# Tile 0 of a linear attention and rational feed-forward kernel: float32 products that read their moving operand plainly

## The chip, the cores and the metric

The kernel runs on one core of one Trainium2 chip. The metric is the device time of that core in microseconds (us), the median of 3 runs. A profiled execution of the same program, taken separately, gives the rows that are quoted below.

## The reference

q, k and v have the shape (batch 8, heads 8, sequence 576, head width 64). The result is 4608 tokens by 512 columns, float32.

```python
kv = np.einsum('bhsd,bhse->bhde', k, v)
out = np.einsum('bhsd,bhde->bhse', q, kv)
rms = np.sqrt(np.mean(out * out, axis=-1, keepdims=True) + 1e-06)
x = out / rms * g_norm                      # then laid out as (4608, 512)
h = x @ w_in                                # (512, 2048)
P = a[0] + a[1] * h + a[2] * h**2 + a[3] * h**3
Q = 1.0 + np.abs(b[0]) * np.abs(h) + np.abs(b[1]) * h**2
g = P / (Q + 1e-06)
result = (g @ w_out).astype(np.float32)     # (2048, 512)
```

The weights w_in and w_out are float64 and are turned into float32 on the chip.

## The kernel before

The 4608 tokens are worked in 9 tiles of 512 (t), and the 2048 inner columns in 16 chunks of 128 (c). A pair (t, c) is a slot; the slots run in one list, and slot i of tile 0 has c = i. For each slot TensorE makes h, a PSUM tile of 128 inner columns by 512 tokens (gemm1_part), ACT, DVE and POOL turn it into g (ew_a, ew_b, ew_c, ew_d), and TensorE adds the slot's products with w_out to four PSUM banks acc, one for each 128 tokens (gemm2). In turn i TensorE gets gemm2 of slot i-2, the attention steps that prepare the next tile, and gemm1 of slot i+1; in the first four turns gemm1 stands ahead of the attention steps. h has two banks, so gemm1 of slot i+1 waits until slot i-1 has been read for the last time (L511).

The elementwise work of a slot passes to and fro: ACT L501 and L502 read h; DVE L504 and L505; ACT L510; DVE L511; ACT L513 and L514 (a logarithm and an exponential); DVE L520, L521 and L527, which gives g. Between these stand the steps of a plan written by hand (first_tiles, L153 to L178, read by todo at L185): in tile 0 and the start of tile 1 they turn the float64 words of both weight matrices into float32 (scale L209 and L211, shift L232, or L237, add L242) and split them into two float32r parts (cast L249, rest L269). An entry as "add P 5q" names the engine and the turn and place. All engines work their queues in order.

Most products are made of three float32r products of split operands (L493, L558). In tile 0 some are not split and run as float32, which takes two passes over the moving operand, each a record of its own with its own weight load: gemm1 of slots 0 to 3 (unsplit1, L486, 4 products each) and gemm2 of slots 0 to 11 (unsplit2, L551, 4 products each). gemm2 of slots 12 to 15 of tile 0 is split (L558, 12 products each).

The host stores the tokens of each tile of q, and the columns of w_out, with the even ones first and the odd ones behind them. The moving operand is read through strands, which takes column 0, 256, 1, 257 and so on, so that h and acc come out in natural order:

```python
    def strands(f):
        return f.rearrange("p (a b) -> p b a", a=2)
```

Other places read such an operand plainly: the first tile's attention output (first_o, L669, float32) and the later tiles' attention (att_o, L389 to L391, float32r, in two runs of stored order). When a tile's gemm2 is complete, evacuate copies acc to SBUF and stores it; for tile 0 that stands in turn 17 behind gemm2 of slot 15, and all four copies are ACT's (L567). gemm2 of tile 1's first slot (slot 16) writes the same four banks.

Of the kernel before, what the change touches and what calls it, by code (L numbers as in the profile page):

```python
# [23 lines left out]
def linear_attention_then_rational_ffn(  # L24
# [10 lines left out]
    PE, ACT, DVE, POOL = nc.tensor, nc.scalar, nc.vector, nc.gpsimd  # L35

    NB, NPAIR = kv.shape[:2]
    NT, DM = out.shape
    NF = w_in.shape[0]
    P = 128  # L40
# [79 lines left out]
    def unsplit1(t, c):  # L120
        return t == 0 and c < 4
# [4 lines left out]
    def unsplit2(t, c):  # L126
        return t == 0 and c < SPLIT0
# [61 lines left out]
    raws, ups, w32, whl, wparts = {}, {}, {}, {}, {}  # L189
# [130 lines left out]
    kvq, qs, sqs, rs, rbs, xf = {}, {}, {}, {}, {}, {}  # L320
# [52 lines left out]
    def halves(f):  # L373
        return f.rearrange("p (a b) -> p a b", a=2)
# [86 lines left out]
    acc = {}  # L461
# [6 lines left out]
    def in_turn(behind, n):  # L468
        each = [(k, j) for k in range(n) for j in range(3) if j != behind]
        return each if behind is None else each + [(k, behind) for k in range(n)]  # L470

    def strands(f):
        return f.rearrange("p (a b) -> p b a", a=2)

    def gemm1(t, c):
        if t == NTILE - 1 and c % 3 == 2:
            ph = ps_at.tile([P, TW], F32, tag="at", name=f"h_{t}_{c}", bufs=1)
        else:
            ph = ps_h.tile([P, TW], F32, tag="h", name=f"h_{t}_{c}")
        gemm1_part(t, c, ph)  # L480
        return ph

    def gemm1_part(t, c, ph, kcs=range(NPAIR)):
        if unsplit1(t, c):
            for kc in kcs:
                PE.matmul(ph, w32["wi", c][:, kc * P:(kc + 1) * P], strands(xf[t, kc]), start=(kc == 0), stop=(kc == NPAIR - 1))  # L486
            return
        order = in_turn(behind1.get((t, c)), NPAIR)
        for n, (kc, j) in enumerate(order):
            xh, xl = (strands(f) for f in x[t][kc])  # L490
            wh, wl = (f[:, kc * P:(kc + 1) * P] for f in whl["wi", c])
            w, f = ((wh, xh), (wl, xh), (wh, xl))[j]
            PE.matmul(ph, w, f, start=(n == 0), stop=(n == len(order) - 1))  # L493
# [23 lines left out]
    def ew_c(t, c, fill=lambda k: None):  # L517
        q, u, r = pend[t, c]
        fill(0)
        DVE.scalar_tensor_tensor(u, u, na[:, 0:1], r, ALU.add, ALU.mult)  # L520
        DVE.scalar_tensor_tensor(r, q, QEPS, r, ALU.add, ALU.mult)  # L521
        fill(1)
        if unsplit2(t, c):
            g = gs[t, c] = work.tile([P, TW], F32, tag=("gh", "gl")[c % 2], name=f"g_{t}_{c}")
        else:
            g = u
        DVE.scalar_tensor_tensor(g, r, 2.0, u, ALU.subtract, ALU.mult)  # L527
        fill(2)

# [14 lines left out]
    def gemm2(t, c):  # L544
        g = gs.pop((t, c))
        first, last = c == 0, c == NF - 1
        if first:
            acc[t] = [ps_acc.tile([P, DM], F32, tag="acc", name=f"acc_{t}_{s}") for s in range(NSUB)]
        if unsplit2(t, c):
            for s in range(NSUB):  # L550
                PE.matmul(acc[t][s], g[:, s * P:(s + 1) * P], strands(w32["wo", c]), start=first, stop=last)  # L551
            return
        (gh, gl), (wh, wl) = g, whl["wo", c]
        products = (gh, wh), (gh, wl), (gl, wh)
        order = in_turn(behind2.get((t, c)), NSUB)
        for n, (s, j) in enumerate(order):
            a, w = products[j]
            PE.matmul(acc[t][s], a[:, s * P:(s + 1) * P], strands(w), start=first and j == 0, stop=last and all(k != s for k, _ in order[n + 1:]))  # L558

    def evacuate(t):  # L560
        for k in range(NSUB // 2):
            ob = work.tile([P, 2, DM], F32, tag="rb", name=f"ob_{t}_{k}", bufs=2)
            for s in range(2):
                if s and 2 < t + 2 < NB:
                    DVE.tensor_copy(ob[:, s], acc[t][2 * k + s])
                else:
                    ACT.copy(ob[:, s], acc[t][2 * k + s])  # L567
            r0 = t * TW + 2 * k * P
            nc.sync.dma_start(out[r0:r0 + 2 * P].rearrange("(s p) d -> p s d", s=2), ob)

    def finish(t, ph):
# [12 lines left out]
        for k, (v, q, u, gh, gl, r) in zip(parts, halves):  # L584
# [4 lines left out]
            ACT.activation(r, q, AF.Ln, bias=bias[:, 2:3], scale=QSC)  # L589
            ACT.activation(r, r, AF.Exp, bias=bias[:, 3:4], scale=-1.0)  # L590
        gemm2(t, c - 2)
        for v, q, u, gh, gl, r in halves:
            DVE.scalar_tensor_tensor(u, u, na[:, 0:1], r, ALU.add, ALU.mult)
# [173 lines left out]
    scale_low(("wi", 2), ACT, two)  # L767
    h00 = ps_h.tile([P, TW], F32, tag="h", name="h_0_0")
    gemm1_part(0, 0, h00, (0,))
    first_rb(1)  # L770
    first_warm(3, 1)
# [5 lines left out]
    first_norm(3)  # L777
    scale_high(("wi", 2), DVE, two)
    gemm1_part(0, 0, h00, (1,))
    conv_b2(("wi", 0), two)  # L780
    first_rb(2)
# [10 lines left out]
    ph = h00  # L792
# [22 lines left out]
    for i, (t, c) in enumerate(slots[:-1]):  # L815
# [8 lines left out]
        if i >= LAG:  # L824
            gemm2(*slots[i - LAG])
            if slots[i - LAG][1] == NF - 1:
                evacuate(slots[i - LAG][0])
        if i < 4:
            ph = gemm1(0, i + 1)
        if t + 1 < NTILE:  # L830
# [4 lines left out]
            if i == MOVE[0]:  # L835
                last = work.tile([P, 2 * DM], F32, tag="rb", name="w_last", bufs=2)
# [6 lines left out]
        if t == NTILE - 1:  # L843
            ahead += [gemm1(*slots[k]) for k in ((i + 1, i + 2) if c == 0 else (i + 2,)) if k < len(slots)]
            ph = ahead.pop(0) if ahead else None
        elif i >= 4:
            ph = gemm1(*slots[i + 1])
        if c == NF - 2 and 0 < t < NTILE - 1:
            xl = [split(t + 1, p) for p in range(NPAIR)]
            for k in range(2):  # L850
                rest[k].append(xl[k])
                rest[2].append(xl[2 + k])
        ew_c(t, c, lambda k: [todo(i, "rgz"[k]), *(f() for f in rest[k])])
    finish(NTILE - 1, ph)

# [43 lines left out]
```

## Time and profile before

| what | value |
|---|---|
| median of 3 runs | 867.98 us (867.84 to 868.21) |
| the profiled execution: its own time, its span | 868.07 us, 866.3 us |
| PE busy, share of the span | 853.2 us, 98% |
| PE weight loads | 696.0 us, 80% |
| DVE | 687.7 us, 79% |
| ACT | 699.3 us, 81% |
| POOL | 328.1 us, 38% |
| granted TensorE clock | 1.000 |

The span goes from the first to the last instruction of the profiled execution; 1.8 us of its own time lie outside. Records of matmuls overlap, because each carries the time in which its results drain: the spacing of their starts is what one costs in a row of several. The chain of waits follows the work that ended last back from the end, at each step to what released it.

### The profile page before, as it was taken

Reading aid. Unit: us, or ns where it says so; the run is one execution under the profiler, and the core shown is the slowest. Engines: PE = TensorE matmul, PEld = TensorE weight load, DVE = VectorE, ACT = ScalarE, POOL = GpSimd, SP = SyncE. Lnnn points to the kernel's source line nnn. Section 1 sums busy time; section 2 is a strip of 40 time slices with the busy share of each in tenths; the row PEclk is TensorE's granted clock in tenths of the full one; section 3 lists DMA queues with packets and bytes.
Section 4 is the critical chain, followed back from the end, with each engine's and each line's share of the span. In section 5 each row is a group of like instructions: output and inputs, shape, how many; then the busy total and the mean of one; then the engine's idle time right before and its main releaser. Section 6 shows DMA issues by size and latency. Waiting matters only on the chain.

```text
span 866.3 us, 11993 instructions
## 1 busy us (share of the span) xinstructions
PE 853.2 (98%) x4370; PEld 696.0 (80%) x4370; DVE 687.7 (79%) x1022; ACT 699.3 (81%) x1129; POOL 328.1 (38%) x265
## 2 busy tenths in 40 slices
PE   8999999999999999999999999999999999999998
PEld 5355558888888888888888888888888888888886
DVE  3989998997887688768876887678877877787886
ACT  5988878897788678868886888868887788778875
POOL 3585555342433242424242423323332434142221
PEclk9999999999999999999999999999999999999999
DMA  9664262114010321132112202020112010101001
GB/s 358 274 250 169 98 213 62 62 37 147 26 61 27 133 50 48 37 135 50 49 37 99 85 3 71 25 50 2 61 37 49 2 61 25 33 18 49 1 1 49
DMA packets 24191, 65.93 MB, mean 76 GB/s; under 512 B 2372, under 2 KB 2756, under 8 KB 24132
## 3 DMA queue, kind: packets, MB, share of 16 engines
q1 hardware_dynamic: 23968, 65.04, 22.1%
q8 instruction: 34, 0.56, 0.3%
q14 instruction: 25, 0.20, 0.1%
q10 hardware_dynamic: 164, 0.14, 0.0%
HBM read 55.59 MB, written 9.57 MB: 75 GB/s over the span
## 4 chain that ended last, share of the span: by engine, by line
PE 61%; DVE 19%; ACT 17%; issue 2%; DMA 1%; SPq 0%; ACTq 0%; DVEq 0%
PE h L493 24%; PE acc L558 21%; PE acc L551 6%; ACT r L513 5%; ACT r L514 4%; DVE u L520 4%; ACT q L510 4%; DVE q L504 4%; DVE r L521 4%; DVE u L527 4%; PE h L486 2%; DVE x L316 2%; PE ms L344 2%; PE ms L410 1%; PE op L391 1%
## 5 line engine op out<-in xcount | busy, mean ns | idle before, releaser
L493 PE MATMUL h<-x,wiparts 128*128 128x512 f32 x1680 | 390.2, 382 | 0.0
L493 PEld LDWEIGHTS h<-x,wiparts 128*128 128x128 f32 x1680 | 315.2, 189 | 50.4 <-issue 4.1
L538 POOL TENSOR_TENSOR gl<-u,gh 128x512 fp32r<-128x512 f32 x131 | 170.7, 1303 | 411.7 <-ACT gh L537 338.1
L520 DVE SCALAR_TENSOR_TENSOR u<-u,na,r 128x512 f32<-128x512 f32 x143 | 106.9, 748 | 81.9 <-ACT r L514 81.5
L504 DVE SCALAR_TENSOR_TENSOR q<-v,b0abs,h 128x512 f32<-128x512 f32 x143 | 106.2, 742 | 57.7 <-ACT u L502 57.1
L501 ACT ACTIVATE v<-h,b 128x512 f32<-128x512 f32 x143 | 98.3, 688 | 55.8 <-PE h L493 53.4
L558 PE MATMUL acc<-woparts,gh 128*128 128x512 f32 x400 | 120.3, 380 | 3.5 <-ACT r L514 2.5
L558 PE MATMUL acc<-woh,gh 128*128 128x512 f32 x320 | 121.3, 379 | 0.0
L558 PE MATMUL acc<-woh,gl 128*128 128x512 f32 x320 | 121.3, 379 | 0.0
L558 PE MATMUL acc<-wol,gh 128*128 128x512 f32 x320 | 118.9, 379 | 0.4 <-POOL wol L269 0.4
L510 ACT ACTIVATE q<-q 128x512 f32<-128x512 f32 x143 | 90.3, 632 | 35.8 <-DVE q L504 33.9
L537 ACT CAST gh<-u 128x512 fp32r<-128x512 f32 x131 | 81.1, 619 | 44.7 <-DVE u L527 44.7
L511 DVE SCALAR_TENSOR_TENSOR u<-u,na,h 128x512 f32<-128x512 f32 x143 | 106.9, 748 | 5.1
L502 ACT ACTIVATE u<-h,na 128x512 f32<-128x512 f32 x143 | 110.9, 776 | 0.0
L513 ACT ACTIVATE r<-q,bias 128x512 f32<-128x512 f32 x143 | 99.1, 693 | 4.5
L521 DVE SCALAR_TENSOR_TENSOR r<-q,r 128x512 f32<-128x512 f32 x143 | 98.8, 691 | 0.0
L514 ACT ACTIVATE r<-r,bias 128x512 f32<-128x512 f32 x143 | 94.7, 662 | 4.6
L505 DVE TENSOR_TENSOR u<-u,h 128x512 f32<-128x512 f32 x143 | 97.4, 681 | 0.0
L527 DVE SCALAR_TENSOR_TENSOR u<-r,u 128x512 f32<-128x512 f32 x131 | 90.5, 691 | 4.2
L558 PEld LDWEIGHTS acc<-woparts,gh 128*128 128x128 f32 x400 | 75.1, 189 | 16.2 <-ACT r L514 4.3
L558 PE MATMUL acc<-woparts,gl 128*128 128x512 f32 x200 | 76.9, 384 | 1.7 <-POOL gl L538 1.5
L558 PEld LDWEIGHTS acc<-wol,gh 128*128 128x128 f32 x320 | 60.5, 189 | 9.3 <-POOL wol L269 0.8
(139 smaller groups left out, 889.0 us busy)
## 6 DMA issues: line engine op xcount, KB each, us to landing
kvm<-in_kv_dram SPq DMA_DIRECT2D x28, 640.0 KB
raw_wo<-in_w_out_dram SPq DMA_DIRECT2D x8, 1024.0 KB
qr<-in_qT_dram SPq DMA_DIRECT2D x32, 256.0 KB
rb<-rd SPq DMA_DIRECT2D x32, 256.0 KB
out_dram<-ob SPq DMA_DIRECT2D x16, 512.0 KB
raw_wi<-in_w_in_dram SPq DMA_DIRECT2D x6, 1024.0 KB
first<-in_first_dram SPq DMA_DIRECT2D x4, 640.0 KB
raw_wi<-in_w_in_dram SPq DMA_DIRECT2D x4, 512.0 KB
```

Of the source, the lines that this page charges most:

```text
L493: PE.matmul(ph, w, f, start=(n == 0), stop=(n == len(order) - 1))
L502: ACT.activation(u, ph, AF.Identity, bias=na[:, 2:3], scale=na[:, 3:4])
L504: DVE.scalar_tensor_tensor(q, v, b0abs, ph, ALU.add, ALU.mult)
L510: ACT.activation(q, q, AF.Abs)
L511: DVE.scalar_tensor_tensor(u, u, na[:, 1:2], ph, ALU.add, ALU.mult)
L513: ACT.activation(r, q, AF.Ln, bias=bias[:, 2:3], scale=QSC)
L514: ACT.activation(r, r, AF.Exp, bias=bias[:, 3:4], scale=-1.0)
L520: DVE.scalar_tensor_tensor(u, u, na[:, 0:1], r, ALU.add, ALU.mult)
L521: DVE.scalar_tensor_tensor(r, q, QEPS, r, ALU.add, ALU.mult)
L527: DVE.scalar_tensor_tensor(g, r, 2.0, u, ALU.subtract, ALU.mult)
L538: POOL.tensor_tensor(gl, u, f32(gh), ALU.subtract)
L558: PE.matmul(acc[t][s], a[:, s * P:(s + 1) * P], strands(w), start=first and j == 0, stop=last and all(k != s for k, _ in order[n + 1:]))
```

## The change

In tile 0 the unsplit gemm1 products read xf plainly, so h of slots 0 to 3 comes out in stored order (even tokens, then odd). L527 of these slots reads its operands in two halves and writes g with a step of two elements, which puts g in natural order. All gemm2 products of tile 0, split ones too, read w_out plainly, so acc of tile 0 comes out in stored order, and the four copies of evacuate for tile 0 read PSUM through strands and write contiguously. Other tiles, and gemm1 of slots 4 to 15, stay as they are.

```diff
     def gemm1_part(t, c, ph, kcs=range(NPAIR)):
         if unsplit1(t, c):
             for kc in kcs:
-                PE.matmul(ph, w32["wi", c][:, kc * P:(kc + 1) * P], strands(xf[t, kc]), start=(kc == 0), stop=(kc == NPAIR - 1))
+                PE.matmul(ph, w32["wi", c][:, kc * P:(kc + 1) * P], xf[t, kc], start=(kc == 0), stop=(kc == NPAIR - 1))
             return
...
             g = u
+        if unsplit1(t, c):
+            g, r, u = g.rearrange("p (b a) -> p a b", a=2), halves(r), halves(u)
         DVE.scalar_tensor_tensor(g, r, 2.0, u, ALU.subtract, ALU.mult)
...
         if unsplit2(t, c):
             for s in range(NSUB):
-                PE.matmul(acc[t][s], g[:, s * P:(s + 1) * P], strands(w32["wo", c]), start=first, stop=last)
+                PE.matmul(acc[t][s], g[:, s * P:(s + 1) * P], w32["wo", c], start=first, stop=last)
             return
...
-            PE.matmul(acc[t][s], a[:, s * P:(s + 1) * P], strands(w), start=first and j == 0, stop=last and all(k != s for k, _ in order[n + 1:]))
+            PE.matmul(acc[t][s], a[:, s * P:(s + 1) * P], strands(w) if t else w, start=first and j == 0, stop=last and all(k != s for k, _ in order[n + 1:]))
...
                 if s and 2 < t + 2 < NB:
                     DVE.tensor_copy(ob[:, s], acc[t][2 * k + s])
+                elif t:
+                    ACT.copy(ob[:, s], acc[t][2 * k + s])
                 else:
-                    ACT.copy(ob[:, s], acc[t][2 * k + s])
+                    ACT.copy(ob[:, s].rearrange("p (b a) -> p b a", a=2), strands(acc[t][2 * k + s]))
```

## Rows read from the trace of the kernel before

**Rows 1.** Chain of waits, 20 to 160 us: shares by line; then start, us, what.

```profile
by line: PE acc L551 37.3%; PE h L493 30.3%; PE h L486 11.8%; PE acc L558 10.8%; PE op L385 2.8%; PE kvp L344 2.1%; PE ms L344 1.9%; PE rb L708 1.3%; PE ms L410 0.7%; PE rb L651 0.6%; DVE xf L711 0.5%; issue 0.0%
...
24.49 11.07 PE h L486 x20
...
147.59 2.59 PE acc L558 x12
```

**Rows 2.** Groups of PE instructions: busy us, mean ns; two records make one float32 product.

```profile
L551 PE MATMUL acc<-wow,g 128*128 128x512 f32 x96 | 54.0, 705 | 0.0
L486 PE MATMUL h<-xf,wiw 128*128 128x512 f32 x32 | 18.2, 710 | 1.1 <-DVE xf L711 1.1
```

**Rows 3.** Timeline of weight loads, one for each float32 pass: start, us, what.

```profile
14.52 0.19 PEld L669 LDWEIGHTS op<-first,kvf 128*128 128x128 f32 x1 [0.24 <-issue]
14.95 0.19 PEld L669 LDWEIGHTS op<-first,kvf 128*128 128x128 f32 x1 [0.24 <-issue]
...
28.91 0.19 PEld L486 LDWEIGHTS h<-xf,wiw 128*128 128x128 f32 x1 [0.35 <-issue]
29.45 0.19 PEld L486 LDWEIGHTS h<-xf,wiw 128*128 128x128 f32 x1 [0.35 <-issue]
```

**Rows 4.** Timeline of PE: three plainly read float32r products, and what follows them.

```profile
712.32 0.40 PE L389 MATMUL op<-qh,kvh 128*128 128x512 f32 x1
...
713.02 2.75 PE L493 MATMUL h<-x,wiparts 128*128 128x512 f32 x12
```

**Rows 5.** Windows, tile 0: PE, PEld, DVE, ACT, POOL busy us (instructions), clock, DMA.

```profile
24.50:132.00 107.50, 107.50 (x416) 56.35 (x417) 100.85 (x126) 90.60 (x136) 67.85 (x40) 1.00 0.53 192
```

**Rows 6.** Timeline of DVE: each wait in tile 0; in brackets idle time and releaser.

```profile
23.74 0.69 DVE L711 TENSOR_TENSOR xf<-xf,rb 128x512 f32<-128x512 f32 x1 [0.39 <-PE rb L708]
...
28.41 0.75 DVE L504 SCALAR_TENSOR_TENSOR q<-v,b0abs,h 128x512 f32<-128x512 f32 x1 [0.15 <-ACT u L502]
...
58.01 0.75 DVE L504 SCALAR_TENSOR_TENSOR q<-v,b0abs,h 128x512 f32<-128x512 f32 x1 [2.45 <-ACT u L502]
...
86.80 0.75 DVE L504 SCALAR_TENSOR_TENSOR q<-v,b0abs,h 128x512 f32<-128x512 f32 x1 [1.34 <-ACT u L502]
...
125.05 0.75 DVE L504 SCALAR_TENSOR_TENSOR q<-v,b0abs,h 128x512 f32<-128x512 f32 x1 [1.15 <-ACT u L502]
```

**Rows 7.** Timeline of ACT: its waits for TensorE ahead of the last three L504.

```profile
53.78 0.20 ACT L274 CAST kvh<-kvp 64x64 fp32r<-64x64 f32 x1 [2.18 <-PE kvp L344]
...
85.41 0.69 ACT L501 ACTIVATE v<-h,b 128x512 f32<-128x512 f32 x1 [2.12 <-PE h L493]
...
123.67 0.69 ACT L501 ACTIVATE v<-h,b 128x512 f32<-128x512 f32 x1 [2.27 <-PE h L493]
```

**Rows 8.** Timeline around the evacuation of tile 0 and gemm2 of slots 16 and 18.

```profile
151.77 2.05 ACT L567 COPY ob<-acc 128x512 f32<-128x512 f32 x4
...
153.91 0.44 PE L558 MATMUL acc<-woparts,gh 128*128 128x512 f32 x1
154.19 0.38 PE L558 MATMUL acc<-woparts,gl 128*128 128x512 f32 x1
...
161.68 1.28 POOL L538 TENSOR_TENSOR gl<-u,gh 128x512 fp32r<-128x512 f32 x1 [4.58 <-issue]
...
163.25 0.38 PE L558 MATMUL acc<-woh,gl 128*128 128x512 f32 x1
```

**Rows 9.** ACT groups (busy us, mean ns): contiguous PSUM, stepped SBUF; then three DVE timeline rows.

```profile
L209 ACT ACTIVATE xf<-op,ghalf 128x512 f32<-128x512 f32 x3 | 2.0, 678 | 0.0
L209 ACT ACTIVATE raw_wi<-raw_wi 128x512 f32<-128x512 f32 x1 | 0.7, 675 | 0.0
...
13.58 0.43 DVE L211 TENSOR_SCALAR raw_wi<-raw_wi 128x512 f32<-128x512 f32 x1 [6.45 <-DMA raw_wi<-in_w_in_dram]
14.57 0.42 DVE L232 TENSOR_SCALAR wiw<-raw_wi 128x512 int32<-128x512 int32 x1
...
60.05 2.10 DVE L232 TENSOR_SCALAR wiw<-raw_wi 128x1024 int32<-128x1024 int32 x1
```

## The prediction, made before the change was run

> **What bounds the kernel now.** I read the chain of waits first. From 24 to 158 us it is TensorE's alone: one matmul group after the other, the unsplit float32 products of the two lines that change holding 49% of it [rows 1]. A shorter product there shortens the span, as long as nothing else is nearly as full. So the second view is the busy time of that window: PE 107.5 of 107.5 us, but DVE 100.85 of the same 107.5 [rows 5]. DVE converts the weights and computes g here, and has 6.65 us of room. The third view is the DVE timeline: what its idle time waits for. Four waits, 0.15, 2.45, 1.34 and 1.15 us, end with ACT L502, in slots 0, 4, 8 and 13 [rows 6], and in the last three ACT had itself been waiting for TensorE for 2.1 to 2.3 us [rows 7]. Those are what a faster TensorE can give back; in the rest of the window DVE works its queue end to end.
>
> **What TensorE saves.** A float32 product is two passes. A pass of the strided reading starts 0.54 us after the one before (28.91 to 29.45), a plainly read one of the same 512 columns 0.43 us (14.52 to 14.95) [rows 3]: 0.11 us less. There are 32 + 96 = 128 passes [rows 2], so 14.1 us. The other way round for the 48 split products of slots 12 to 15: plainly read float32r products take (713.02 - 712.32) / 3 = 0.233 us [rows 4], the strided ones 2.59 / 12 = 0.216 [rows 1]; 48 x 0.017 = 0.8 us dearer, between nothing (if those rows owe it to being in two runs) and 0.8. Net 13.3 us of TensorE's queue. Here a rule bears: the Trainium skill, Advanced Engine Details and Errata, section Memory Cachelines, says that accesses which each fall on another line of SBUF pay a penalty. The float32 rows agree, the float32r rows contradict it; by the rule the 0.8 us would be no cost at all.
>
> **What of it reaches the end.** I follow DVE, since it can't do with less than its work. (1) Ahead of 24.5 us, L711 waits 0.39 us for the rb products, which stand behind an unsplit product; its two passes save 0.22, and DVE's queue starts 0.22 earlier. (2) Slot 0: 0.15 goes, as the first h is done earlier; 0.37 in all. (3) Slot 4: ACT waits 2.18 us for kvp, since that stands on TensorE behind gemm2 of slot 1 and gemm1 of slot 4. Those come some 3 us earlier: 32 passes of gemm1 and 16 of gemm2 have gone by, 48 x 0.11 = 5.3 us, of which TensorE gives part back waiting for slot 0's L511 to free a bank of h and for g of slot 1. ACT then runs 0.37 + 2.18 = 2.55 us earlier, and DVE's 2.45 shrinks to what ACT still leaves: shift 2.55. (4) Slot 8: 1.34, as ACT's 2.12 is longer and h is by then early enough: 32 + 7 x 8 = 88 passes have gone by, 9.7 us, less some 2 that TensorE waits before; 3.89. (5) Slot 13: 1.15, ACT's 2.27 again being longer; 5.04. (6) Slot 17: a last 0.1 to 0.15. DVE, ACT and POOL end tile 0 about 5.2 us earlier.
>
> TensorE could be 13.3 us early and is held to this. It will wait some 8 us in tile 0, in pieces: for L511 of slot 0, for g of slots 1, 5 and 9, at the ms products for ACT's squares, and most in turn 14, where gemm2 of slot 12 needs DVE's low part of the weights (L269). Behind these the second gate is the evacuation. Four ACT copies, 2.05 us, free the banks that gemm2 of slot 16 writes, and the last pair of rows (153.91 to 154.19 instead of 0.22 apart) shows that TensorE already waits 0.06 us for the fourth [rows 8]; so it can gain there what ACT gained, 5.2, and no more. In slot 18 gl ends at 161.68 + 1.28 = 162.96, and TensorE takes it at 163.25 [rows 8]: 0.29 us to spare, so 5.2 passes. After that each tile repeats and everything is moved by the same amount.
>
> **The two strided accesses.** L527 of slots 0 to 3 writes with a step of two, on the engine that will be the bound. DVE with the same step in and out takes 0.43 us for 512, with a contiguous output 0.42 [rows 9]: I take nothing. The other end is a doubling; at the 0.75 us of an L504, an instruction of the same kind and size [rows 6], 4 x 0.75 = 3.0 us, of which some 0.2 hides ahead of slot 4. In between lies the 26% that the strided pass costs TensorE (0.54 against 0.43), 0.8 us. A gain is excluded, since the present write is contiguous already. The evacuating copies read PSUM with a step of 256 elements, which no row shows for ACT. A step of two in SBUF costs it nothing (675 against 678 ns) [rows 9]: I take nothing here too; the copies take 2.05 / 4 = 0.51 us each [rows 8]; 26% would be 0.13 each, 0.5 in all, a doubling 2.0. Nothing hides this: h of slot 18 is read behind the copies, and the banks come free with them. LDWEIGHTS of g, the stores and every DMA stay as they were. SP's fetches of qr wait for att_o products, which come earlier, so nothing moves back.
>
> **Sum.** 868.07 - 5.2 = 862.9 us against the profiled execution, which is 0.09 above the median: 862.8 us.
>
> **Rivals.** *The whole 13.3 us arrive*, 854.7. For it: the chain shows TensorE alone. Against: DVE would have to do 100.85 us of work in 94. Chance 0.04. *A strided access is dearer than its nearest row*: the evacuation at double cost leaves 5.2 - 2.0 = 3.2, 864.8; the DVE write at double cost 5.2 - 2.8 = 2.4, 865.6; both at 26% leave 5.2 - 0.6 - 0.5 = 4.1, 863.9. For it: TensorE pays for the same step. Against: the stepped ACT and DVE rows. Chance 0.18. The Trainium skill's same section gives PSUM lines of 8 bytes, by which each element of these copies is on a line of its own; no run here shows it for ACT, and the doubling stands for it. *The passes don't get shorter*: strided and plain passes would be 0.54 because of their stage, not their reading. Against: the plain rows stand a few us away at the same clock. No change, 868.0; chance 0.08. *Slower*: the same four copies at a far larger price, in turn 17 on ACT. Each us there delays slot 18 and gemm2 of slot 16 alike; from 5.2 / 4 = 1.3 us more per copy (0.5 to 1.8) the gain is gone, and at five times the present price, 2.5, it is 4 x 2.0 - 5.2 = 2.8 us slower, 870.8. For it: no row has this access. Against: even TensorE's step of 256 costs a quarter. Chance 0.06. The forecast has 0.64.
>
> **How the numbers follow.** A run of this kernel can tell about 0.2%, 1.7 us, from no change. The forecast, nearly all of the dearer accesses and the full gain are faster by more: 0.64 + 0.17 + 0.04 = 0.85. Within 0.2% are the unshortened passes and a doubling of both accesses, 0.09; slower 0.06. The low end of the range is a gain of 7 us: a DVE shift takes 0.42 us for 512 words at one place and 2.10 for 1024 at another [rows 9], by what runs beside it, so that a new alignment can be worth some 2 us; 860.8. The high end holds each dearer access alone with some more, a gain of 1.8, 866.2. Outside are 0.04 + 0.08 + 0.06 and little else.
>
> **What would show it.** Weight loads of L486 and L551 0.43 us apart; DVE's waits for ACT L502 in slots 4, 8 and 13 gone or small, and its idle time in tile 0 under 2 us; new idle time of PE of some 8 us before slot 16, released by DVE, ACT and POOL; the four copies still 2.05 in all; and gemm2 of slot 18 some 5 us earlier than before, with the same distance from there to the end. I am wrong if PE has no new waits, if L567 or the first four L527 are longer, or if DVE's work in tile 0 isn't about 100 us.

## The result: 860.9 us for 867.9, and the profile after

The changed kernel takes 860.88 us (median of 4 runs, 860.71 to 860.92), the kernel before 867.91 beside it: a ratio of 0.9918 (95% interval 0.9904 to 0.9933), 7.0 us less. The forecast was 862.8, a gain of 5.2. The direction was as forecast, and DVE takes over from TensorE as forecast, though with ACT in slots 4 to 8, which was not. The forecast gain was 1.8 us too small, and the experiments are mostly about these 1.8.

The line of busy times of the changed kernel (PE was 853.2, DVE 687.7, ACT 699.3 before):

```profile
PE 841.8 (98%) x4370; PEld 695.4 (81%) x4370; DVE 685.1 (80%) x1022; ACT 698.9 (81%) x1129; POOL 327.9 (38%) x265
```

Four lines are inserted along the way: L486 keeps its number, L527 is now L529, L551 is L553, L558 is L560, and tile 0's copies are L571.

First the change itself, in the groups of PE (to be held against [rows 2]) and in two weight loads (against [rows 3]):

```profile
L553 PE MATMUL acc<-wow,g 128*128 128x512 f32 x96 | 43.5, 595 | 0.7 <-POOL wow L242 0.7
L486 PE MATMUL h<-xf,wiw 128*128 128x512 f32 x32 | 14.9, 604 | 1.6 <-DVE xf L715 1.1 <-DVE u L511 0.5
```

```profile
36.75 0.19 PEld L553 LDWEIGHTS acc<-wow,g 128*128 128x128 f32 x1 [0.24 <-PE acc L553]
37.18 0.19 PEld L553 LDWEIGHTS acc<-wow,g 128*128 128x128 f32 x1 [0.24 <-issue]
```

A pass is 0.43 us instead of 0.54, and the two groups lose 10.5 and 3.3 us. Both had no idle time for want of an elementwise engine before, apart from the 1.1 at the start; now they have.

Next the chain of waits from 20 to 160 us, which was TensorE's alone from 24 us on [rows 1] (start, duration, what; the longest pieces):

```profile
15.90 15.75 DMA raw_wi<-in_w_in_dram
31.73 1.17 ACT raw_wi L209
...
61.26 1.65 ACT raw_wi L209
...
87.94 1.23 DVE wiw L237
...
133.10 1.06 DVE x L316
134.69 2.97 PE acc L560 x12
```

It begins with a load of weights that lands at 31.7 us, runs over ACT and DVE through tile 0, with ACT's weight scalings (L209) in slots 4 to 8, and comes back to TensorE only at 134.7 us.

The windows show where the time went. They hold the same 143 DVE instructions of tile 0 and the start of tile 1, first before, then after (columns as in [rows 5]):

```profile
24.20:143.90 119.70, 119.41 (x504) 66.63 (x505) 112.11 (x143) 101.47 (x154) 76.62 (x45) 1.00 0.51 182
```

```profile
23.95:136.95 113.00, 108.52 (x506) 66.33 (x507) 109.59 (x143) 101.04 (x154) 76.55 (x45) 1.00 0.54 196
```

The window is 6.7 us shorter. DVE's idle time fell from 119.70 - 112.11 = 7.6 us to 113.00 - 109.59 = 3.4, by 4.2. The other 2.5 us are in its busy time: **the same 143 instructions took 2.5 us less**. TensorE, which was idle for 0.3 us here before, now is for 4.5. The table of DVE's and of PE's waits in tile 0 names them (us in total, times, longest):

```profile
DVE u L520 <- ACT r L514: 1.7, 3, 0.7
DVE q L504 <- ACT u L502: 0.6, 2, 0.4
```

```profile
PE op L385 <- ACT kvf L275: 1.4, 1, 1.4
PE acc L560 <- POOL gl L540: 1.0, 1, 1.0
PE h L486 <- DVE xf L715: 0.8, 1, 0.8
PE acc L553 <- POOL wow L242: 0.7, 1, 0.7
```

The waits of [rows 6] for ACT L502 in slots 0, 4, 8 and 13 (5.1 us) are gone; two small new ones, 0.43 in slot 1 (behind the late load) and 0.20 in slot 7, make the 0.6.

How much earlier a slot's first DVE step (L504) starts than in the kernel before, in us, is the ledger for everything that follows. Each is read from the profiled execution of its kernel. The rows of the experiments are here too:

| kernel | slot 4 | 8 | 9 | 13 | 14 | 17 | 20 |
|---|---|---|---|---|---|---|---|
| the forecast | 2.55 | 3.89 | 3.89 | 5.04 | 5.04 | 5.2 | 5.2 |
| the change | 2.28 | 4.36 | 5.22 | 6.27 | 6.87 | 7.16 | 7.17 |
| gemm1 part alone | 2.38 | 2.61 | 2.64 | 2.61 | 2.61 | 2.61 | 2.60 |
| gemm2 part alone | 2.10 | 4.32 | 5.27 | 6.40 | 6.99 | 7.28 | 7.28 |
| 14 unsplit slots | 2.74 | 4.73 | 5.64 | 6.67 | 8.65 | 8.93 | 8.93 |
| plain split gemm1 to slot 11 | 2.41 | 5.31 | 7.08 | 8.61 | 9.20 | 9.50 | 9.49 |

From slot 17 on the lead of the change is constant: each later tile repeats it, and it reaches the end whole.

### The profile page after: what moved, and what is told of

It is laid out like the page before. It is cut to its first block, busy times and chain, and to the rows that moved or that the text cites. A ratio compares the mean times of both kernels' runs of the same rounds, so it can differ in the third digit from the quotient of the medians.

```text
span 859.1 us, 11993 instructions
## 1 busy us (share of the span) xinstructions
PE 841.8 (98%) x4370; PEld 695.4 (81%) x4370; DVE 685.1 (80%) x1022; ACT 698.9 (81%) x1129; POOL 327.9 (38%) x265
## 4 chain that ended last, share of the span: by engine, by line
PE 47%; DVE 26%; ACT 21%; issue 3%; DMA 2%; POOL 1%; ACTq 0%; DVEq 0%; POOLq 0%
PE h L493 21%; PE acc L560 20%; DVE u L520 5%; ACT r L513 5%; ACT q L510 5%; ACT r L514 5%; DVE q L504 5%; DVE r L521 4%; DVE u L529 4%; DVE x L316 2%; DMA raw_wi<-in_w_in_dram 2%; PE ms L344 1%; ACT u L502 1%; ACT v L501 1%; PE op L391 1%
## 5 line engine op out<-in xcount | busy, mean ns | idle before, releaser
L493 PE MATMUL h<-x,wiparts 128*128 128x512 f32 x1680 | 390.1, 382 | 0.2 <-DVE x L316 0.2
L493 PEld LDWEIGHTS h<-x,wiparts 128*128 128x128 f32 x1680 | 315.1, 189 | 50.2 <-issue 3.4
L520 DVE SCALAR_TENSOR_TENSOR u<-u,na,r 128x512 f32<-128x512 f32 x143 | 106.7, 746 | 82.0 <-ACT r L514 81.7
L504 DVE SCALAR_TENSOR_TENSOR q<-v,b0abs,h 128x512 f32<-128x512 f32 x143 | 106.1, 742 | 53.3 <-ACT u L502 52.6
L560 PE MATMUL acc<-woparts,gh 128*128 128x512 f32 x400 | 121.1, 382 | 3.8 <-ACT r L514 2.5
L560 PE MATMUL acc<-woh,gh 128*128 128x512 f32 x320 | 121.3, 379 | 0.0
L560 PE MATMUL acc<-woh,gl 128*128 128x512 f32 x320 | 121.3, 379 | 0.0
L560 PE MATMUL acc<-wol,gh 128*128 128x512 f32 x320 | 118.9, 379 | 0.4 <-POOL wol L269 0.4
L502 ACT ACTIVATE u<-h,na 128x512 f32<-128x512 f32 x143 | 110.9, 776 | 0.0
L529 DVE SCALAR_TENSOR_TENSOR u<-r,u 128x512 f32<-128x512 f32 x131 | 90.5, 691 | 4.2
L560 PEld LDWEIGHTS acc<-woparts,gh 128*128 128x128 f32 x400 | 74.9, 189 | 17.5 <-ACT r L514 4.3
L560 PE MATMUL acc<-woparts,gl 128*128 128x512 f32 x200 | 77.2, 386 | 2.6 <-POOL gl L540 2.5
L560 PEld LDWEIGHTS acc<-wol,gh 128*128 128x128 f32 x320 | 60.5, 189 | 9.3 <-POOL wol L269 0.8
```

The costliest lines, as they stand in the source:

```text
L502: ACT.activation(u, ph, AF.Identity, bias=na[:, 2:3], scale=na[:, 3:4])
L504: DVE.scalar_tensor_tensor(q, v, b0abs, ph, ALU.add, ALU.mult)
L560: PE.matmul(acc[t][s], a[:, s * P:(s + 1) * P], strands(w) if t else w, start=first and j == 0, stop=last and all(k != s for k, _ in order ...
```

## The experiments

The theory at the start was that DVE and ACT set the pace of tile 0 once TensorE is faster. Its rivals: that TensorE still does, that the strided accesses cost part of the gain, and, for the unforeseen 2 us, that DVE's work is not a constant. Each ratio below is to the kernel before, run beside it (its medians lie between 867.78 and 868.06). A comparison with the changed kernel's 860.88 goes across sessions, and executions of one kernel lie up to 1.8 us apart, so a difference of under 1 us to it says little by itself.

**One part alone.** In one kernel the gemm2 products and the copies stay as before, in the other gemm1 and L527 do.

```diff
-                PE.matmul(acc[t][s], ..., w32["wo", c], ...)
+                PE.matmul(acc[t][s], ..., strands(w32["wo", c]), ...)
```

> Only the 32 passes of gemm1 are read plainly, with g of slots 0 to 3 put in order by the stepped write; gemm2 and the evacuation stay as before. If DVE is the second bound, TensorE is 3.5 us early at most and DVE gives back what it waited for up to that: nearly all of 2.45 in slot 4 and little later, 2.5 to 3.2 us in all, about 865.2. If TensorE alone set the time, 32 x 0.11 = 3.5 us, 864.4. If the stepped write of g cost DVE something, under 2 us.

> Only gemm2 of tile 0 (96 passes and the 48 split products) is read plainly, with the evacuation that goes with it; gemm1 stays as before. If TensorE alone set the time, 96 x 0.11 - 0.8 = 9.8 us, 858.1. If DVE is the second bound: 16 passes have gone by ahead of the kvp of slot 3, so 1.8 of the 2.45 us go there, then 1.34 and 1.15 and the rest of the first, 4.5 to 5.2 us, about 863. If most of the gain beyond the waits comes from how DVE's and POOL's work happen to lie beside each other, the result is up to 2 us off that, to either side, and this run and the one with gemm1 alone don't add up to the whole change.

Measured: 865.41 us for gemm1 alone (ratio 0.9972, 0.9961 to 0.9983), 860.99 for gemm2 alone (0.9923, 0.9907 to 0.9940). The parts give 2.4 and 6.8, together 9.2, where the whole change gives 7.0: by the table each gives back slot 4's wait on its own. gemm2 alone gives the whole gain, and missed its expectation by the same 2 us as the forecast did.

**The strided accesses undone.** L529 and the four copies of tile 0 work contiguously, so tile 0 comes out in stored order.

```diff
-        if unsplit1(t, c):
-            g, r, u = g.rearrange("p (b a) -> p a b", a=2), halves(r), halves(u)
...
-                    ACT.copy(ob[:, s].rearrange("p (b a) -> p b a", a=2), strands(acc[t][2 * k + s]))
+                    ACT.copy(ob[:, s], acc[t][2 * k + s])
```

> The changed kernel with g of slots 0 to 3 written contiguously and the evacuation of tile 0 read contiguously (the order of those tokens and columns is left as stored). If the two strided accesses cost nothing, as forecast, within 0.3 us of the changed kernel, 860.9; at 26% each, 1 us less; doubled, 2 to 4 us less.

Measured: 860.78 us (0.9921, 0.9906 to 0.9935), no change, as forecast. The changed kernel's own rows say the same, one strided L529 (of slot 1; those of slots 2 and 3 take 0.74 and 0.75, which is taken up below) and the four copies, which took 2.05 us before too [rows 8]:

```profile
41.18 0.69 DVE L529 SCALAR_TENSOR_TENSOR g<-r,u 128x512 f32<-128x512 f32 x1
...
144.59 2.05 ACT L571 COPY ob<-acc 128x512 f32<-128x512 f32 x4
```

**DVE's work taken away.** If DVE bounds the changed kernel and TensorE the one before, less DVE work shortens the one and not the other. First the OR (L237) of five of w_out's eight units is left out:

```diff
+        if u[0] == "wo" and 2 <= u[1] <= 10:
+            return
         DVE.scalar_tensor_tensor(w, high, -(1 << 31), w, ALU.bitwise_and, ALU.bitwise_or)
```

> The kernel before without five of DVE's instructions in tile 0 (L237 of w_out's chunks 2 to 10, which puts the signs in; so those weights keep no sign): 6.8 us of DVE's work. If TensorE bounds tile 0 before the change, as its chain says, the time moves by less than 0.7 us: about 867.6. If DVE were the bound already, some 5 us less.

> The changed kernel without the same five instructions of DVE (the same weights keep no sign): 6.5 us of its work. If DVE is the bound of tile 0 after the change, most of it shows, up to what TensorE still has (13.3 less the 7.0 measured): 4 to 6 us, 855 to 857. If TensorE or the evacuation holds the changed kernel, under 1 us.

Measured: 868.60 us on the kernel before (1.0009, 1.0000 to 1.0018), 859.60 on the changed one (0.9908, 0.9893 to 0.9923). TensorE as the bound before is confirmed: with less work for DVE the time didn't fall. After, only 1.3 of some 6 us of work came through, far from the expected 4 to 6. DVE's waits for ACT L502 rose from 0.6 to 3.6 us, so the step "follow DVE" is too simple: in slots 4 to 8 ACT is full as well.

**POOL's adds taken away.** This was the first test of DVE's conversions waiting for POOL: L242 of 12 of the 16 units is left out, which is POOL's work alone.

```diff
+        if by == POOL and u not in (("wi", 0), ("wi", 2), ("wo", 0)):
+            return
         by.tensor_tensor(w, w, low, ALU.add)
```

> The kernel before without POOL's additions of the low words in tile 0 (L242 for all but the first chunks; the weights lose their low bits): 12 instructions of about 2.4 us of POOL's time, none of DVE's. TensorE still bounds tile 0: the time moves by less than 0.7 us. DVE's busy time in tile 0 should fall by 3 us or more if its instructions are longer because POOL works beside them, and stay within 1 us if not.

> The changed kernel without the same additions of POOL. If DVE bounds tile 0 and its conversions are longer because of POOL, the time falls by 3 to 5 us, to 856 to 858, though DVE's instructions are the same in number. If DVE's durations don't depend on POOL, under 0.7 us.

Measured: 868.24 us before (1.0005, 0.9996 to 1.0015), 860.14 after (0.9912, 0.9897 to 0.9926). DVE's 143 instructions got faster without being touched, 112.11 to 110.55 us before (1.6, between the expectation's two cases) and 109.59 to 106.48 after (3.1). The end gained only 0.7, too little to be told from no change across sessions: DVE does depend on POOL, and ACT again held slots 4 to 8 (slot 8 is 4.48 us ahead of the kernel before, for 4.36).

**ACT's scalings of the low words left out too,** and then the ORs as well, all on the changed kernel:

```diff
+        if engine == ACT and u not in (("wi", 0), ("wi", 2), ("wo", 0), ("wo", 12)):
+            return
         low = words(u, part)[0]
```

> The changed kernel without POOL's additions, as in the run before (860.1), and also without ACT's scaling of the low words that they would have added (L209, 10 instructions of about 1.15 us; the weights lose their low bits). In that run no slot from 4 to 8 came earlier than in the changed kernel, with the chain of waits on ACT there. If ACT is the bound of slots 4 to 8, L504 of slot 8 now comes 2 us or more earlier than without the additions alone and the time falls by 1 to 3 us, to 857 to 859. If DVE alone is the bound, under 0.5 us.

> The same, and also without the five L237 of DVE (no signs on those weights): work taken from POOL, ACT and DVE together. If the changed kernel is held by ACT in slots 4 to 8 and by DVE from slot 8 on, each alone gave 0.7 to 1.3 us because the other stayed, and the three together give much more than their sum: 855 to 857, with TensorE the bound again, near 868.0 - 13.3 = 854.7 as the floor. If the gate is the evacuation or TensorE, the sum of the parts, about 858.

Measured: 861.03 us (0.9921, 0.9906 to 0.9936), no gain with less work on two engines where 857 to 859 was expected, and 857.43 (0.9878, 0.9862 to 0.9895) with less on three, just above the expected 855 to 857. The first is a miss that teaches: the timeline of DVE and POOL shows two DVE steps landing right behind a POOL instruction that has just begun (L320 and L239 are the kernel's L316 and L237, four and two lines further down; L273 is L269).

```profile
41.72 2.68 DVE L320 TENSOR_TENSOR x<-xf,x 128x512 fp32r<-128x512 f32 x1
55.40 3.35 DVE L239 SCALAR_TENSOR_TENSOR wow<-raw_wo,wow 128x1024 int32<-128x1024 int32 x1
...
41.50 2.35 POOL L273 TENSOR_TENSOR wiparts<-wiw,wiparts 128x1024 fp32r<-128x1024 f32 x1 [0.55 <-ACT wiparts L253]
55.30 2.37 POOL L273 TENSOR_TENSOR wiparts<-wiw,wiparts 128x1024 fp32r<-128x1024 f32 x1 [1.33 <-DVE r L525]
```

POOL ends at 43.85 and 57.67; the DVE steps end at 44.40 and 58.75, that is 0.55 and 1.08 later, what such a step takes when POOL is idle (0.68 and 1.22) less 0.14. So two steps of together 1.9 us took 6.0.

**Steps moved, no work changed.** This is the direct test. In the changed kernel one step waits in this way (DVE, then POOL):

```profile
44.42 2.45 DVE L237 SCALAR_TENSOR_TENSOR wiw<-raw_wi,wiw 128x1024 int32<-128x1024 int32 x1
46.79 0.74 DVE L520 SCALAR_TENSOR_TENSOR u<-u,na,r 128x512 f32<-128x512 f32 x1
...
43.24 2.37 POOL L269 TENSOR_TENSOR wiparts<-wiw,wiparts 128x1024 fp32r<-128x1024 f32 x1 [1.44 <-ACT wiparts L249]
45.56 3.56 POOL L242 TENSOR_TENSOR wow<-wow,raw_wo 128x1024 int32<-128x1024 int32 x1
```

L237 begins at 44.42, POOL's L269 ends at 45.61, L237 1.26 later; and POOL's next add, in turn, takes 3.56 instead of some 2.4, since it stands behind L237. L520 beside the rest of that add takes its usual 0.74: one of its two operands, r, lies in PSUM. One entry of the plan moves L237 ahead, to where POOL is idle (place h of a turn comes before place e, so the "later" of the expectation is a slip, and its L239 is L237):

```diff
-        ("wi", 6): "... or D 2e, ..."
+        ("wi", 6): "... or D 2h, ..."
```

> The changed kernel with one DVE step of the plan (the OR, L239 there, of weight chunk 6 of w_in) issued half a turn later, at about 42.4 us, where POOL is idle; nothing is added or left out. If DVE's operations of two SBUF operands wait for the POOL instruction that is running when they begin (in the changed kernel this one takes 2.45 us, 43.24 to 45.61 being POOL's), it takes 1.22 us here and DVE's first step of slot 3 begins some 1.2 us earlier (47.6 for 48.8 us); the end stays within 0.3 us, because ACT sets the pace in slots 4 to 8. If the 2.45 us is the operation's own work at this place, its duration and slot 3 stay as they are.

Measured: 862.40 us (0.9938, 0.9923 to 0.9953), 1.5 slower than the changed kernel; no execution of the one overlaps the other's. DVE, then POOL:

```profile
42.18 1.22 DVE L237 SCALAR_TENSOR_TENSOR wiw<-raw_wi,wiw 128x1024 int32<-128x1024 int32 x1
46.17 0.75 DVE L520 SCALAR_TENSOR_TENSOR u<-u,na,r 128x512 f32<-128x512 f32 x1 [0.74 <-ACT r L514]
50.55 2.69 DVE L232 TENSOR_SCALAR wow<-raw_wo 128x1024 int32<-128x1024 int32 x1
55.27 2.40 DVE L237 SCALAR_TENSOR_TENSOR wow<-raw_wo,wow 128x1024 int32<-128x1024 int32 x1
...
50.32 2.37 POOL L269 TENSOR_TENSOR wiparts<-wiw,wiparts 128x1024 fp32r<-128x1024 f32 x1
54.19 2.40 POOL L269 TENSOR_TENSOR wiparts<-wiw,wiparts 128x1024 fp32r<-128x1024 f32 x1 [0.37 <-POOL kvl L280]
```

The step takes 1.22, as the theory said and its rival did not. The expected start of slot 3 and the expected end were wrong: slot 3 begins 0.3 us earlier and not 1.2, since the place that the step left is now a wait of 0.74 for ACT, and two later steps fall behind POOL instructions, 2.69 and 2.40 us for 1.17 and 1.68 in the changed kernel. With the same 143 instructions DVE is busy for 1.1 us more:

```profile
23.90:138.50 114.60, 108.52 (x506) 66.31 (x507) 110.72 (x143) 101.27 (x154) 74.32 (x45) 1.00 0.54 193
```

The second kernel of this kind moves three steps out of POOL's way:

```diff
-  ("wi", 14): "... lo D 8v, ..."     ("wo", 10): "... shift D 9e, ..."     ("wo", 12): "... shift D 11e, ..."
+  ("wi", 14): "... lo D 8g, ..."     ("wo", 10): "... shift D 9g, ..."     ("wo", 12): "... shift D 11g, ..."
```

> The changed kernel with three DVE steps of the plan issued a little later in their turns (low part of chunk 14 of w_in in turn 8, shifts of chunks 10 and 12 of w_out in turns 9 and 11), with the same work. They begin behind a running POOL instruction in the changed kernel and take 1.76, 1.53 and 1.09 us; alone such steps take 0.68. If POOL's running instruction is what they wait for, they are 0.7 to 0.9 us each here, the sum of DVE's busy time in tile 0 falls by some 2 us, and since DVE sets the pace from slot 8 on, the run ends 1.1 to 2.2 us earlier: 858.7 to 859.8. If the durations are the steps' own, nothing changes: 860.7 to 861.0.

Measured: 862.70 us (0.9943, 0.9930 to 0.9955), 1.8 slower than the changed kernel where 1.1 to 2.2 faster was expected. DVE, then POOL:

```profile
83.99 2.16 DVE L237 SCALAR_TENSOR_TENSOR wow<-raw_wo,wow 128x1024 int32<-128x1024 int32 x1
89.18 0.76 DVE L211 TENSOR_SCALAR raw_wi<-raw_wi 128x1024 int32<-128x1024 uint32 x1
109.42 0.69 DVE L232 TENSOR_SCALAR wow<-raw_wo 128x1024 int32<-128x1024 int32 x1
110.62 2.58 DVE L237 SCALAR_TENSOR_TENSOR wow<-raw_wo,wow 128x1024 int32<-128x1024 int32 x1
...
82.47 2.40 POOL L269 TENSOR_TENSOR wiparts<-wiw,wiparts 128x1024 fp32r<-128x1024 f32 x1 [1.93 <-ACT wiparts L249]
110.56 1.29 POOL L269 TENSOR_TENSOR wiparts<-wiw,wiparts 128x512 fp32r<-128x512 f32 x1 [2.70 <-ACT wiparts L249]
```

The moved steps take 0.76, 0.69 and 0.69, as expected, but the next step in the queue inherits the wait (2.16 for 1.19), and one falls behind POOL at 110.56. Durations follow POOL's instructions; which kernel is faster cannot be told from one of them. In all 20 traces together, 141 of DVE's conversion steps with 1024 columns (between 24 and 144 us) begin behind a POOL instruction, with more than 0.14 us of it left, and meet no split gemm1 product (L493): each takes its own time plus what is left of that instruction, less 0.12 to 0.14 us, without exception.

**Two ideas for a shorter tile 0.** In four kernels more of gemm2 is unsplit, so that the split of w_out's last units is needed a tile later; one moves a low part from DVE to POOL.

```diff
-    SPLIT0 = 12
+    SPLIT0 = 16
...
-        ("wo", 12): "... cast A 13h, rest D 13r",
+        ("wo", 12): "... cast A 16h, rest P 16g",
-        ("wo", 14): "... cast2 D 15h, cast1 A 15v, rest P 15g",
+        ("wo", 14): "... cast A 18h, rest P 18g",
```

> The changed kernel with gemm2 of slots 12 to 15 of tile 0 unsplit too, and the casts and rests of w_out's chunks 12 to 15 put off into tile 1 (rests on POOL). It takes four casts and the low parts of g and 1.2 us of DVE's L269 out of the end of tile 0, where DVE is the bound, for 4 x (3.44 - 2.8) = 2.6 us more of TensorE, which had waits there. If DVE's chain sets the end of tile 0, 0.8 to 2 us less than the changed kernel, 859 to 860; if TensorE is near its limit again, slower by up to 1 us.

> The changed kernel with one step of slot 7, the low part of w_in's first chunks (L269, 1.22 us on DVE), given to POOL. DVE gets 1.2 us less work just ahead of slot 8. If DVE is the bound from slot 8 on and ACT up to it, it shows only as far as ACT lets slot 8 start earlier: 0 to 0.5 us; POOL's 2.4 us can hold up a conversion of DVE that starts beside it, so up to 1 us slower is possible.

Measured: 862.68 us (0.9941, 0.9926 to 0.9956) and 860.98 (0.9920, 0.9905 to 0.9935; a low part of w_in's first unit, turn 7, on POOL): the first 1.8 slower than the changed kernel, the second no different. In the first, DVE led by 9.0 us at slot 16 and lost 3.3 of it in slots 17 to 19, where a low part on DVE waits 1.1 us for ACT's cast. So the casts were put on DVE (16v and 19v) and their low parts on POOL (16g and 19g), alone and with the three moves above:

> The changed kernel with all 16 of tile 0's gemm2 slots unsplit, so that the split of chunks 12 to 15 of w_out is needed a tile later, and those casts and low parts placed on DVE and POOL in turns 16 and 19, where DVE has idle time. The same casts on ACT and in turns 16 and 18 cost more than they gave in the run before of this kind (862.68). If it was their place that cost, this ends at about 859; if tile 0's end is set by TensorE once more, because 16 unsplit products of 1.73 us stand in place of 12 split ones of 2.6 to 3.0, it gains up to 2 us of TensorE's queue and the end moves by what DVE and ACT leave of it, 859 to 860.5.

> The kernel before this one in the list together with the three moved DVE steps of the one before that. If both theories hold, their gains add, 857 to 858; if the three moved steps do nothing, it is as the kernel without them.

Measured: 860.99 us (0.9923, 0.9909 to 0.9936) and 861.52 (0.9929, 0.9917 to 0.9942): neither gains on the changed kernel. The first was expected at 859 to 860.5; the second comes out near what was expected if the moves do nothing. Of the first one's lead of 9.2 us at slot 16, slots 17, 21 and 26 lost 2.1. An unsplit slot costs TensorE 8 x 0.43 = 3.4 us, a split one, plainly read, 12 x 0.233 = 2.8, and ACT waits 1.3 us for TensorE's h of slot 17. Hence 14 instead of 16, with only unit 12's split put off (cast D 16v, rest P 16g):

> The changed kernel with gemm2 of slots 12 and 13 of tile 0 unsplit too (14 slots instead of 12), and the cast and low part of chunk 12 of w_out in turn 16 on DVE and POOL. With all 16 unsplit DVE was 9.2 us ahead of the kernel before at slot 16, and the end lost 1.0 of it to TensorE (an unsplit slot costs 8 x 0.43 = 3.4 us, a split one 12 x 0.233 = 2.8) and 0.7 to a low part placed on POOL in turn 19. Here TensorE has half of the first loss and none of the second. If that is what the end lacked, 859.0 to 859.8; if tile 0's end is held by DVE and ACT as in the changed kernel whatever is unsplit, 860.5 to 861.0.

Measured: 859.28 us (0.9901, 0.9884 to 0.9917), within the expectation and 1.6 us below the changed kernel. The two intervals overlap, but every execution of this kernel (859.17 to 859.38) lies below every one of that (860.71 to 860.92).

**Steps that are longer though POOL is idle.** Over the 18 traces up to here, 285 conversion steps of DVE with 1024 columns ran while POOL was idle. The 194 with no split gemm1 product (L493) beside them, or for at most 0.11 us, took 0.69 or 1.22 us to within 0.05. Of the 52 that had such products beside them for nine tenths of their time or more, the 48 that read the float64 words, 4 bytes of every 8, took 0.15 to 0.52 us more, 0.27 in the mean; the 4 that read contiguous float32 took at most 0.02 more. ACT behaves alike: L209, which reads the same words, took 1.47 to 1.78 us in 63 such places and 1.13 to 1.28 in 203 without; its casts L249, which read contiguously, took 1.02 to 1.10 in both. The step that writes g (L529) took 0.75 to 0.86 in 11 places where it writes with a step of 8 bytes beside such products, and 0.69 to 0.71 in 28 with none; with a contiguous write it takes 0.69 beside them too. So in these traces only the two together stretch a step: split products that TensorE reads with a step, and a neighbour that itself reads or writes with one. The same three scalings of L209, of slots 4 to 7, before and after:

```profile
63.18 1.16 ACT L209 ACTIVATE raw_wi<-raw_wi 128x1024 int32<-128x1024 uint32 x1
72.06 1.16 ACT L209 ACTIVATE raw_wi<-raw_wi 128x1024 int32<-128x1024 uint32 x1
78.82 1.16 ACT L209 ACTIVATE raw_wi<-raw_wi 128x1024 int32<-128x1024 uint32 x1
```

```profile
61.13 1.78 ACT L209 ACTIVATE raw_wi<-raw_wi 128x1024 int32<-128x1024 uint32 x1
69.73 1.65 ACT L209 ACTIVATE raw_wi<-raw_wi 128x1024 int32<-128x1024 uint32 x1
76.43 1.63 ACT L209 ACTIVATE raw_wi<-raw_wi 128x1024 int32<-128x1024 uint32 x1
```

Before, they lie beside unsplit float32 products, which were read through strands too and stretch nothing; after, beside split ones. These split products still read x through strands. The test lets them read plainly wherever gemm2 is unsplit (slots 4 to 11), and g of those slots is put in order as in slots 0 to 3. The same edit was made on the kernel with 14 unsplit slots.

```diff
-            xh, xl = (strands(f) for f in x[t][kc])
+            xh, xl = x[t][kc] if unsplit2(t, c) else (strands(f) for f in x[t][kc])
...
-        if unsplit1(t, c):
+        if unsplit2(t, c):
             g, r, u = g.rearrange("p (b a) -> p a b", a=2), halves(r), halves(u)
```

> The changed kernel with the split gemm1 products of slots 4 to 11 reading x plainly too (g of these slots is written with a step of two, as in slots 0 to 3). In the traces so far ACT's scalings L209 take 1.16 us alone and 1.61 to 1.78 where split gemm1 products run beside them (61.13, 69.73, 76.43 and 83.75 in the changed kernel, slots 4 to 8, where ACT sets the pace), and DVE's steps are stretched by 0.2 to 0.5 in the same company. If the products' strided reading causes it, L209 takes about 1.16 in these places, slots 5 to 8 begin 1 to 2 us earlier, and the end moves by 0.4 to 1.9 us, 859.0 to 860.5, give or take the 1.5 us that a new alignment with POOL can be worth. If split products stretch their neighbours whichever way they read, L209 stays at 1.6 in these places and the time at 860.5 to 861.3.

> The same edit on the kernel with 14 unsplit slots (859.28), here for slots 4 to 13. If the strided reading stretches ACT's and DVE's steps, 857.4 to 858.9; if it does not, 859.0 to 859.7.

Measured: 858.30 us (0.9887, 0.9870 to 0.9903) and 858.53 (0.9890, 0.9875 to 0.9905), both as expected if the strided reading is the cause. In the first (ACT, then TensorE):

```profile
60.74 1.18 ACT L209 ACTIVATE raw_wi<-raw_wi 128x1024 int32<-128x1024 uint32 x1
68.71 1.15 ACT L209 ACTIVATE raw_wi<-raw_wi 128x1024 int32<-128x1024 uint32 x1
75.12 1.18 ACT L209 ACTIVATE raw_wi<-raw_wi 128x1024 int32<-128x1024 uint32 x1
82.80 1.14 ACT L209 ACTIVATE raw_wi<-raw_wi 128x1024 f32<-128x1024 f32 x1
...
68.22 3.27 PE L493 MATMUL h<-x,wiparts 128*128 128x512 f32 x12
82.52 3.26 PE L493 MATMUL h<-x,wiparts 128*128 128x512 f32 x12
```

```profile
23.90:134.50 110.60, 109.06 (x506) 66.12 (x507) 107.39 (x143) 98.98 (x155) 76.82 (x45) 1.00 0.55 200
```

L209 is back at its own time, also where split products lie beside it from start to end (68.71 and 82.80; the latter took 1.61 at 83.75 in the changed kernel). Slots 5 to 9 gain 0.5 to 1.9 us on the changed kernel, and DVE's 143 instructions take 107.4 us for 109.6. The strided reading of those products was what stretched ACT and DVE. TensorE's idle time in the window is down to 1.5 us, so it is again close to the bound. In the kernel with both edits, worth 1.6 and 2.6 alone, it is the bound: its chain of waits is TensorE's alone from 30 us on, TensorE has no wait of 0.15 us or more between 31 and 150 us, and ACT waits for h of slots 16 and 17. That is why the two don't add up.

```profile
132.61 0.69 ACT L501 ACTIVATE v<-h,b 128x512 f32<-128x512 f32 x1 [0.98 <-PE h L493]
...
137.93 0.69 ACT L501 ACTIVATE v<-h,b 128x512 f32<-128x512 f32 x1 [0.57 <-PE h L493]
```

The 858.30 is the fastest kernel here that computes everything, 2.6 us below the changed one and 9.7 below the one before.

## Why the prediction was right, and where it was wrong

**What bounds.** Right for the kernel before: TensorE alone (leaving out DVE or POOL work there gave nothing). Right in part for the changed one: DVE, as forecast, but ACT in slots 4 to 8.

**What TensorE saves.** Right: 0.43 for 0.54 us in each of the 128 passes. The split products at 0.233 us were 0.8 dearer, as forecast. The forecast idle time of "some 8 us" measured 4.5, and at partly other places (1.4 for ACT's L275, 1.0 for gl in turn 14, where L269 was named and cost 0.3); this step was not needed for the sum.

**What reaches the end.** The four waits went as listed, in slots 0, 4, 8 and 13. DVE's idle time gave back 4.2 us in the window, 0.3 ahead of it and 0.2 in slot 17, 4.7 in all, about the forecast 5.2 less the two new waits of 0.6. With the 2.5 us of busy time this makes the 7.2 by which the profiled executions' spans differ.

**The step that failed** is "I follow DVE, since it can't do with less than its work", and with it "in the rest of the window DVE works its queue end to end". DVE's busy time was taken as its work, and a part of it was waiting and stretching, of which the change took away 2.5 us. The table shows it: the lead grows by 0.86 us at slot 9 and by 0.60 at slot 14, where DVE had no wait to give back. The 35 conversion steps with 1024 columns between 24 and 144 us took 11.4 us more than they take alone before, and 8.7 after. The measure of the 141 steps above tells the two causes apart. Waiting for a POOL instruction in progress came to 8.1 us before and 6.7 after. The rest, the stretching beside the strided split products, came to 3.3 and 2.0 (and to 0.2 in the kernel with 858.30). So of the 2.7 us that these steps lost, 1.4 were waits for POOL and 1.2 were stretching; DVE's other instructions make up the small difference to 2.5.

The low end of the range rested on such an effect, "by what runs beside it", and put it at 2 us, but as a possibility and not as a term: that the low end, 860.8, comes near the measured 860.9 is owed to this allowance and not to the sum. To forecast the sign and size, each step would have had to be placed against POOL's and TensorE's instructions after the change, and the two moved-step kernels show how easily such a placing goes wrong. But that DVE's 100.85 us were not all work was there to be read, in [rows 9]: 2.10 us for a shift, beside this row of POOL in the kernel before,

```profile
59.13 2.42 POOL L242 TENSOR_TENSOR wow<-wow,raw_wo 128x1024 int32<-128x1024 int32 x1
```

which ends at 61.55, 0.60 ahead of the shift's end at 62.15.

A second thing was not seen: that ACT is full in slots 4 to 8. The new alignment puts its scalings beside split products there (1.61 to 1.78 for 1.16 us), and taking work from DVE alone gave little. Nor is the way there a sum of waits: at slot 3 the lead was -0.05 us, not 0.37, as L237 had just stood behind POOL for 1.2 us (44.42), and at slot 4 it was 2.28.

**The strided accesses** cost next to nothing, as taken: the copies nothing, the stepped write of g 0.05 us in each of slots 2 and 3. The rivals of dearer accesses, of unshortened passes and of a slower kernel are out, and so are the whole 13.3 us. **The evacuation** was as forecast: four copies, 2.05 us.

## What to carry to other kernels

Busy time in a profile is not always work: hold an operation's longest duration against its shortest, and look at what the other engines run at that moment, before calling an engine full. When a change shifts engines against each other, the waits inside their operations move too, here by up to 2 us in either direction without any work changed, so a forecast that only adds up idle times carries that much uncertainty. Where TensorE's float32r operands can be read plainly and the order mended in a write elsewhere, neighbours that read or write with a step gain as well.

## What the hardware showed that was not expected

DVE's weight conversions wait, counted as busy, until the POOL instruction in progress ends: shifts and scalings with one operand (0.69 us alone, up to 2.69) and steps with two operands in SBUF (1.22 alone, up to 3.35). The wait is what is left of POOL's instruction less 0.12 to 0.14 us, in all 141 steps counted above. Steps with one operand in PSUM don't wait: L520 takes 0.74 with POOL running and without. The Trainium skill, SBUF — State Buffer, section Who interferes with whom, has a rule for it: DVE and GpSimd share one pair of ports, and whichever instruction comes first holds it to its end. The rows above agree in both directions, DVE behind POOL (2.45) and POOL behind DVE (3.56).

The same section says that "PE and ACT never wait on anyone", and names no contention but that of the shared pair. The runs here differ: beside float32r products that TensorE reads with a step, ACT's L209 took up to 1.78 us for 1.16 and DVE's steps up to 0.52 more with POOL idle, and reading those products plainly removed it for both (L209 1.14 to 1.18, DVE's stretching 0.2 us for 2.0). Only steps that themselves read or write with a step of 8 bytes were stretched.

The reading order's own cost to TensorE depends on the type: strided float32 passes take 0.54 us for 0.43, strided float32r products 0.216 for 0.233.
